# Two-word exponential on VectorE, Q and K through HBM: an attention and long-convolution kernel on one core

## The chip, the cores and the metric

The kernel runs on one core of one Trainium2 chip. The metric is the device time of one execution in microseconds: 822.26 us is the median of three runs (822.12 to 822.35). The engines of the core are named as in the profile: PE (TensorE), DVE (VectorE), ACT (ScalarE), POOL (GpSimd) and SP (SyncE, which here only issues transfers).

## The reference

Two independent halves are computed and laid side by side. S = 2048, D = 640, all tensors bf16.

```python
# half A: short causal filter of k over 4 taps, times v, then a causal long filter per channel
for t in range(4):
    k_shift = k_shift + k_pad[:, t:t + S, :] * shift_k[:, 3 - t]
kv = k_shift * v
y = irfft(rfft(kv, 2S) * rfft(ssm_k, 2S))[:S] + kv * ssm_D
a = q * y
# half B: attention, 32 heads of 20
qkv = x @ wqkv
p = softmax(einsum("bhqd,bhkd->bhqk", q, k) * 20 ** -0.5)
b = einsum("bhqk,bhkd->bhqd", p, v) @ wo
out = concatenate([a, b], axis=-1)
```

## The kernel before

**Attention.** The 32 heads lie in 8 groups of 4. A tile is one group and 512 queries; there are 32 tiles, and a tile has 16 key blocks of 128. One score block is one head, 128 keys and 512 queries: 2,048 of them, numbered in order (four heads, then the next key block). A score block is one matmul with K as weights (L630, 20 x 128) and Q streaming; three neighbouring heads run side by side in three row strips of the array and write three PSUM banks. Banks 0 to 2 and 3 to 5 take turns. ACT turns two or three banks into bf16 exponentials with one instruction (L672), written to a pool of 44 slots of 512 columns (`P_sb`).

Some third banks go to DVE (298 blocks): L692 turns the score into a 16-bit integer that is a rough bf16 power of two (`XV`), and for two such blocks together a chain corrects the mantissa: L727 masks its 7 bits, L728, L729, L730 and L732 form a polynomial, and L722 (both blocks in one instruction) or L724 (one each) adds it to the integer. The result is one bf16 slot.

PV multiplies the exponentials of a key block by V with a column of ones (L750, four heads side by side in four column strips) and sums over the 16 key blocks in bank 6. The tile is copied out (L761), transposed, divided by its sums (L782, L784), and once all groups of a query range are there, multiplied by wo (L831, L847).

**Projections.** x comes transposed by DMA into `xT`. Q and K of one group and 512 positions are one task: five steps of four matmuls side by side (L485) and a copy to `QT` or `KT` (L474); 62 such tasks, and the first two in halves. V of one key block and 8 heads is five matmuls (L531) and a copy (L536): 64 tasks.

**Half A.** The short filter runs on PE with diagonal weights (L560), DVE multiplies by v (L581), and the product kv goes to HBM (`kvr_scratch`), eight transfers of 80 columns for each of 16 row blocks. The long filter is 40 tasks of 128 small matmuls on PE (L1025), 32 to 60 columns each, with windows of the filter loaded from HBM (`hk_load`, 640 transfers) and kv read back (`kvr_load`) and rearranged by POOL (L997). DVE sums (L1041, L1042, L1044), POOL multiplies by q (L1064).

**The order of the work** is written by the builder: `Prog` records each engine's instructions with the semaphores they wait for, and a loop walks along PE's stream. At each point it decides, from costs and ready times that it keeps for all engines, whether the next score group fits, which side task (projection, short filter, output) with a due time to slip in, a convolution piece, PV, or filler matmuls on zeros (`fill`, L391), which are given where PE has streamed too little in the last 3.4 us. `want_vec` decides whether a group's third block goes to DVE. On the chip each engine only follows its list in order.

Of the kernel before, what the change touches and what calls it, by code (L numbers as in the profile page):

```python
# [11 lines left out]
S = 2048  # L12
# [12 lines left out]
NHK = 4  # L25
NAQ = 3
NPU, NPX = 44, 0
# [6 lines left out]
NXB = 3  # L34
KBV, KBW, LONE = 12, 12, 24
CQ, CQD, ZDU = 0.0258, 0.0304, 2.1
KV0, KVS, VQ, CONVE, ZTH, AGE, WAIT3 = 20, 1.7, 5.5, 230, 2.2, 40, 0.2
ZST = 7, 4
DOV, DDEP, SWITCH = 0.085, 0.03, 0.105


EXP_C = (0.07826797, 0.30457564)
# [240 lines left out]
def build_kernel(nc, A_q, A_k, A_v, A_shift_k, A_ssm_k, A_ssm_D, B_x, B_wqkv, B_wo, out):  # L283
# [3 lines left out]
    with ExitStack() as es:  # L287
# [18 lines left out]
        XV_sb = sb("XV", [128, NXB, 1024], U16)  # L306
        XF_sb = sb("XF", [128, 2, 2, 1024])
# [49 lines left out]
        kvr_d = nc.dram_tensor("kvr_scratch", (8, 32, 64, 80), BF16).ap()  # L357

        b_ident, b_ones, b_ZS, b_Dg, b_SK = (Buf() for _ in range(5))
# [5 lines left out]
        b_XF, b_XQ = [Buf(), Buf()], [Buf(), Buf()]  # L365
        b_XV = [[Buf(), Buf()] for _ in range(NXB)]
# [87 lines left out]
        def spare(now):  # L454

            if nu[0] < NPAIR - 6:
                return [MISC] + [OBANK] * (npv[0] == 0 and nu[0] < OBS) + [4, 5]
            side = [2, 5] if nu[0] < NU - 8 and nu[0] >= NPAIR else []
            return side + [MISC] * (not conv_wants(now))
# [7 lines left out]
        npv = [0]  # L467
# [45 lines left out]

        def qs(qc, g):
            return POS[(g, qc)] % NQS
# [7 lines left out]
        VZ = [(0, 8), (8, 8), (16, 8), (24, 8)]  # L523

        def V_task(kb, z, bk):
            h0, nh = VZ[z]
            w = nh * DH
            rd = [b_xT[kb], b_Wa if z == 0 else b_Wb]
            for cc in range(NCC):
                yield (w / 2400 + 0.003, rd if cc == 0 else [])  # L530
                P.op("pe", lambda e, cc=cc: e.matmul(  # L531
                    bank[bk][:, 0:w], xT[:, cc, kb * 128:(kb + 1) * 128],
                    WKV[:, cc, D + h0 * DH:D + h0 * DH + w],
                    start=(cc == 0), stop=(cc == NCC - 1), skip_group_check=True),
                    reads=rd, writes=[bkb[bk]], tok=(cc == NCC - 1), c=w / 2400 + 0.003, st=w / 2400)
            work(1, [(lambda e: e.tensor_copy(V_sb[:, kb, h0 % 16:h0 % 16 + nh, 0:DH],  # L536
                                              bank[bk][:, 0:w].rearrange("p (h d) -> p h d", d=DH)),
                      [bkb[bk], b_ones], [b_V[(kb, z)]], 0.16 + w / 960, False)])
# [11 lines left out]
        def C_task(c, h, bk):  # L550
# [18 lines left out]
            def after():  # L569
                if h < 4:  # L570
                    return
                for t in range(4):
                    bd = Buf()
                    P.dmas("sp", [(ap(kvr_d, [[80, 4], [-5120, 32], [1, 80]], ((32 * n + 31) * 64 + 16 * c + 4 * t) * 80),
                                   kvst[i][:, t, 80 * n:80 * n + 80]) for n in range(8)], d_kvst[4 * i + t], reads=[b_kvst[i]], writes=[bd])
                    b_kvd.append(bd)
                if c < 2:
                    k_load(c + 2)
                    done.add(("L", c + 2))

# [56 lines left out]
        slot, free = {}, set(range(NPX, NPU))  # L637

# [16 lines left out]
        def room(n, vec):  # L655
            a = alloc(n - vec)
            if a is None:
                return None
            if not vec:
                return [a + i for i in range(n)]  # L660
            got = [a + i for i in range(n - vec)]
            free.difference_update(got)
            z = alloc(1)
            free.update(got)
            return None if z is None else got + [z]

        def EXP_task(k, m, vec, b0, got):
            free.difference_update(got)
            for i, z in enumerate(got):
                slot[k + i] = z  # L670
# [4 lines left out]
                reads=[bkb[b0 + i] for i in range(m)], writes=[b_P[z] for z in got[:m]], c=0.066 + 0.4217 * m)  # L675
            if vec:
                chain_start(k + m, b0 + m, got[m])

        chains = []
        xfree = list(range(NXB))  # L680
        nvec = [0, 0]

        opened = []

        def chain_start(n, bk, z):

            nvec[0] += 1
            if not opened:
                opened[:] = [xfree.pop(0), n]
            i, h = opened[0], len(opened) - 2  # L690
            V = XV_sb[:, i, 512 * h:512 * h + 512]
            work(0.2, [(lambda e: e.tensor_scalar(V, bank[bk], scale * 1.4426950408889634 * 128.0, 127.0 * 128.0, op0=ALU.mult,  # L692
                                                  op1=ALU.add), [bkb[bk]], [b_XV[i][h]], 0.684, False)])
            b_P[z].q.append((opened, True))
            opened.append(z)
            if h:
                chain_end()

        def chain_end():

            i, n, zs = opened[0], opened[1], opened[2:]
            opened.clear()
            m = len(zs)
            f = nvec[1] % 2
            nvec[1] += 1
            V, F, Q = XV_sb[:, i, 0:512 * m], XF_sb[:, f, 0, 0:512 * m], XF_sb[:, f, 1, 0:512 * m]
            bv, bf, bq = b_XV[i][0:m], b_XF[f], b_XQ[f]
            a, b = EXP_C
            one, two = 0.154 + 0.1335 * m, 0.154 + 0.267 * m

            def end():
                chains.remove(me)
                xfree.append(i)

# [757 lines left out]
```

## Time and profile before

| what | value |
|---|---|
| median of the runs | 822.26 us |
| profiled execution, its own time | 820.03 us |
| its span | 818.2 us, mean granted clock of PE 0.999 |
| ACT | 800.8 us busy, 750 exponentials (500 of two blocks, 250 of three) |
| DVE | 785.8 us busy, 298 blocks of exponential |
| PE | 796.5 us busy, 11,743 matmuls |
| POOL | 96.4 us busy |
| DMA | 163,226 packets, 121.94 MB, 149 GB/s on average |

A row of the groups reads: line, engine, operation, output and input tile, partitions x elements and type, count, busy us in all, mean ns of one, then the idle time just before these and what ended it. "PEld" is the loading of weights. Successive instructions overlap on an engine, so a mean duration is longer than what one more instruction costs.

### The profile page before, as it was taken

How to read it: one execution, taken by the hardware profiler on the slowest of the kernel's cores; microseconds unless marked ns; L12 is line 12 of the kernel's file. 1: busy time of each engine (PE TensorE's matmuls, PEld its weight loads, DVE VectorE, ACT ScalarE, POOL GpSimd, SP SyncE). 2: the span in 40 equal slices, each digit the busy share in tenths (PEclk: the TensorE clock that was granted, in tenths of full speed). 3: DMA queues.
4: the chain of work that ended last, by engine and by line, in shares of the span. 5: the costliest groups of instructions: out<-in, count | busy, mean ns of one | idle time of the engine just before them, and what ended most of it. 6: DMA issues, size and time to landing. Idle time of an engine off the chain costs nothing.

```text
span 818.2 us, 27604 instructions
## 1 busy us (share of the span) xinstructions
PE 796.5 (97%) x11743; PEld 367.6 (45%) x11743; DVE 785.8 (96%) x1646; ACT 800.8 (98%) x758; POOL 96.4 (12%) x167
## 2 busy tenths in 40 slices
PE   8999999999999999999999999999999999999997
PEld 3444442254545454444454454454444454444332
DVE  2999999999999999999999999999999999999996
ACT  5999999999999999999999999999999999999996
POOL 3000000211010012210001121000111301000110
PEclk9999999999999999999999999999999999999999
DMA  8935423769897889574887778755995968951221
GB/s 181 307 79 94 80 49 52 160 135 195 171 207 159 195 189 204 136 182 111 192 184 165 166 175 190 160 141 118 191 189 135 207 151 180 193 134 46 67 54 37
DMA packets 163226, 121.94 MB, mean 149 GB/s; under 512 B 72832, under 2 KB 161408, under 8 KB 162848
## 3 DMA queue, kind: packets, MB, share of 16 engines
q1 hardware_dynamic: 160912, 117.06, 65.9%
q0 software_dynamic: 736, 2.75, 0.9%
q8 instruction: 93, 1.52, 0.9%
q10 hardware_dynamic: 1456, 0.37, 0.2%
q14 instruction: 29, 0.24, 0.1%
HBM read 106.83 MB, written 10.61 MB: 144 GB/s over the span
## 4 chain that ended last, share of the span: by engine, by line
ACT 43%; DVE 36%; PE 19%; issue 1%; DMA 1%; DVEq 0%
ACT R L672 42%; DVE XV L692 9%; PE PS L630 6%; PE PS L1025 4%; DVE XF L732 4%; DVE XF L729 4%; PE PS L485 3%; DVE R L722 2%; PE PS L750 2%; DVE XF L730 2%; DVE XF L728 2%; DVE XF L727 2%; DVE R L724 2%; DVE R L1044 1%; DVE ZS L1042 1%; DVE ZS L1041 1%
## 5 line engine op out<-in xcount | busy, mean ns | idle before, releaser
L672 ACT ACTIVATE R<-PS 128x1024 bf16<-128x1024 f32 (+1 forms) x750 | 796.6, 1282 | 2.5 <-PE PS L630 1.9
L630 PE MATMUL PS<-QT,KT 20*128 20x512 bf16 x2048 | 291.9, 384 | 10.3 <-ACT R L672 5.5
L692 DVE TENSOR_SCALAR XV<-PS 128x512 uint16<-128x512 f32 x298 | 201.7, 683 | 3.3 <-PE PS L630 1.8
L1025 PEld LDWEIGHTS PS<-R 128*128 128x128 bf16 x5120 | 162.6, 97 | 78.6 <-issue 77.9
L1025 PE MATMUL PS<-R 128*128 128x32 bf16 (+5 forms) x5120 | 196.6, 184 | 0.0
L750 PE MATMUL PS<-R,V_sb 128*21 128x512 bf16 x2048 | 157.5, 383 | 2.6 <-DVE R L722 1.0
L630 PEld LDWEIGHTS PS<-QT,KT 20*128 20x128 bf16 x2048 | 73.0, 91 | 187.9 <-ACT R L672 150.3
L732 DVE TENSOR_TENSOR XF<-XF 128x1024 bf16<-128x1024 bf16 (+1 forms) x155 | 102.5, 661 | 0.3
L729 DVE TENSOR_TENSOR XF<-XF 128x1024 bf16<-128x1024 bf16 (+1 forms) x155 | 102.3, 661 | 0.2
L997 POOL COPY R<-R 128x256 uint32<-128x256 uint32 x80 | 51.1, 639 | 398.5 <-DVE XV L692 144.5
L730 DVE TENSOR_SCALAR XF<-XF 128x1024 bf16<-128x1024 uint16 (+1 forms) x155 | 63.4, 410 | 0.2
L750 PEld LDWEIGHTS PS<-R,V_sb 128*21 128x21 bf16 x2048 | 35.0, 89 | 63.2 <-issue 32.2
L728 DVE TENSOR_SCALAR XF<-XF 128x1024 bf16<-128x1024 uint16 (+1 forms) x155 | 62.4, 407 | 0.2
L727 DVE TENSOR_SCALAR XF<-XV 128x1024 uint16<-128x1024 uint16 (+1 forms) x155 | 62.0, 408 | 0.1
L722 DVE TENSOR_TENSOR R<-XF,XV 128x1024 uint16<-128x1024 bf16 x90 | 61.4, 682 | 0.2
L391 PE MATMUL PS<-Zt 128*128 128x512 bf16 x199 | 58.1, 392 | 1.5 <-DVE Zt L385 1.0
L485 PE MATMUL PS<-xT,WQ 128*20 128x512 bf16 (+1 forms) x660 | 49.6, 375 | 1.7 <-DVE XV L692 0.7
L1064 POOL TENSOR_TENSOR R<-R 128x160 bf16<-128x160 bf16 x64 | 31.2, 487 | 165.1 <-DVE XV L692 48.8
L485 PE MATMUL PS<-xT,WKV 128*20 128x512 bf16 (+1 forms) x660 | 47.9, 375 | 0.1
L724 DVE TENSOR_TENSOR R<-XF,XV 128x512 uint16<-128x512 bf16 x118 | 45.6, 416 | 0.1
L531 PE MATMUL PS<-WKV,xT 128*128 128x160 bf16 x320 | 37.1, 235 | 1.2 <-DVE XV L692 0.8
L531 PEld LDWEIGHTS PS<-WKV,xT 128*128 128x128 bf16 x320 | 21.2, 97 | 22.4 <-issue 11.3
(58 smaller groups left out, 354.7 us busy)
## 6 DMA issues: line engine op xcount, KB each, us to landing
R<-kext_scratch SPq DMA_DIRECT2D x640, 136.0 KB, 3.7
R<-in_A_v_dram SPq DMA_DIRECT2D x4, 640.0 KB, 4.7
kext_scratch<-in_A_ssm_k_dram POOLq DMA_DIRECT2D x1, 2560.0 KB, 13.3
kvr_scratch<-R SPq DMA_DIRECT2D x128, 20.0 KB
R<-kvr_scratch SPq DMA_DIRECT2D x8, 320.0 KB, 5.6
R<-in_A_q_dram SPq DMA_DIRECT2D x32, 80.0 KB, 3.6
out_dram<-R SPq DMA_DIRECT2D x32, 80.0 KB, 3.0
R<-kvr_scratch SPq DMA_DIRECT2D x8, 240.0 KB, 4.9
```

The source lines that it names most:

```text
L485: ins = e.matmul(bank[bk][32 * i:32 * i + DH, 0:n], Wt[:, cc, off + i * DH:off + (i + 1) * DH], xT[:, cc, x0:x0 + n], start=(cc == 0), sto ...
L630: ins = e.matmul(bank[b0 + i], KT[32 * u:32 * u + DH, g % 2, kb * 128:(kb + 1) * 128], QT[32 * u:32 * u + DH, qs(qc, g), :], start=True, s ...
L672: P.op("act", lambda e: e.activation(P_sb[:, s0:s0 + m, :], PS[:, b0 * 512:(b0 + m) * 512].rearrange("p (u q) -> p u q", u=m), ACT.Exp, sc ...
L692: work(0.2, [(lambda e: e.tensor_scalar(V, bank[bk], scale * 1.4426950408889634 * 128.0, 127.0 * 128.0, op0=ALU.mult, op1=ALU.add), [bkb[b ...
L722: last = [(lambda e: e.tensor_tensor(o, Q2, V2, ALU.add), bv + [bq], [b_P[z] for z in zs], two, True)]
L727: (lambda e: e.tensor_scalar(F.bitcast(U16), V, 127, None, op0=ALU.bitwise_and), bv, [bf], one, True),
L728: (lambda e: e.tensor_scalar(Q, F.bitcast(U16), -128.0, None, op0=ALU.add), [bf], [bq], one, True),
L729: (lambda e: e.tensor_tensor(Q, Q, F.bitcast(U16), ALU.mult), [bf, bq], [bq], two, True),
L730: (lambda e: e.tensor_scalar(F, F.bitcast(U16), a / 16384.0, b / 128.0, op0=ALU.mult, op1=ALU.add), [bf], [bf], one, True),
L732: (lambda e: e.tensor_tensor(Q, Q, F, ALU.mult), [bf, bq], [bq], two, True)] + last, end)
L750: ins = e.matmul(bank[OBANK][32 * u:32 * u + DH + 1, :], V_sb[:, kb, (4 * g + u) % 16, :], P_sb[:, slot[4 * b + u], :], start=first, stop= ...
L1025: P.op("pe", lambda e, o=o, lhsT=lhsT, rhs=rhs, st=st, k=k: e.matmul(o, lhsT, rhs, start=st, stop=k == 7, skip_group_check=True), reads=rd ...
```

## The change

- **Exponential on DVE.** The first step writes the 16-bit integer (with another constant) straight into a slot of `P_sb`. For two such blocks together three steps follow: the mantissa with the exponent of 0.5 into `XM`; the exponent with a fixed small mantissa into a second slot; and the first slot times `XM` in place. The sum of the two slots is the exponential; it is never formed, since PV multiplies both by V. `P_sb` has 46 slots, and the block that goes to DVE can be any of the three.
- **PV** is kept as a list per head (`pvq`) and a group takes one item of each head, so that heads with more words than others can be joined freely.
- **Q and K of groups 1 to 6** are computed in chunks of 120 columns (`X_task`: five full matmuls, one copy to `St`), stored to HBM (`qk_scratch`) and loaded back into the four row strips (`KQ_load`). Groups 0 and 7 keep the old tasks.
- **V** of groups 2 to 7 is done for three key blocks in a task and one copy; of groups 0 and 1 for one or two.
- **kv** is stored by whole rows of 640 columns, one transfer for each of 16 row blocks, and loaded in pieces of 80 columns. The loads of the next k and v are issued ahead of the stores.
- Six convolution windows are buffered for four; the constants of the order are others, and the convolution is spread to 160 blocks before the end (230 before). A late side task or convolution piece may be put ahead of a score group.

```diff
-NHK = 4
+NHK = 6
 NAQ = 3
-NPU, NPX = 44, 0
+NPU, NPX = 46, 0
 NQS = 6
 NU = NB * 4
 NPAIR = 8
 VEND = 16
 MM = 0.5
 OBS = 28
-NXB = 3
-KBV, KBW, LONE = 12, 12, 24
+NXB = 2
+KBV, KBW, LONE = 13, 13, 12
 CQ, CQD, ZDU = 0.0258, 0.0304, 2.1
-KV0, KVS, VQ, CONVE, ZTH, AGE, WAIT3 = 20, 1.7, 5.5, 230, 2.2, 40, 0.2
+KV0, KVS, VQ, CONVE, ZTH, AGE, WAIT3 = 20, 1.7, 4, 160, 2.2, 40, 0.6
 ZST = 7, 4
+XG, NXC, NST = 6, 4, 2
+XDL = ((14, 7), (30, 12)), ((70, 8), (90, 12)), ((176, 12), (226, 12)), ((250, 10), (294, 10))
+VBAL = 0
+BEH, BX = 0.5, 0.3
+WAITA, VGAP, SDUE = 0.2, 0, 1.0
 DOV, DDEP, SWITCH = 0.085, 0.03, 0.105
...
-EXP_C = (0.07826797, 0.30457564)
+EXP_C = 127.0 * 128.0 - 76.4457
...
+        def X_task(w, c, t, bk):
+            o = 80 + 120 * c
+            Wt = (WKV, WQ)[w]
+            rd = b_xT[4 * t:4 * t + 4] + [b_Wb] + [b_Wa] * (c == 0)
+            for cc in range(NCC):
+                yield (0.216, rd if cc == 0 else [])
+                P.op("pe", lambda e, cc=cc: e.matmul(bank[bk][0:120, :], Wt[:, cc, o:o + 120], xT[:, cc, 512 * t:512 * t + 512],
+                                                     start=(cc == 0), stop=(cc == NCC - 1), skip_group_check=True),
+                     reads=rd, writes=[bkb[bk]], tok=(cc == NCC - 1), c=0.216, st=0.213)
+            i = nst[0] % NST
+            nst[0] += 1
+
+            def store():
+                P.dma("sp", qk_d[w, 120 * c:120 * c + 120, 512 * t:512 * t + 512], St[0:120, i, :], d_st[i],
+                      reads=[b_St[i]], writes=[b_qk[(w, c, t)]])
+                done.add(("S", w, c, t))
+            work(1, [(lambda e: e.tensor_copy(St[0:120, i, :], bank[bk][0:120, :]), [bkb[bk]], [b_St[i]], 0.69, False)], store)
...
+        def KQ_load(w, g, c):
+            cs = sorted(set((80 * (g - 1) + x) // 120 for x in (0, 79)))
+            ts = range(4) if w == 0 else [c]
+            rd = [b_qk[(w, x, t)] for x in cs for t in ts]
+            pairs = []
+            for u in range(4):
+                r = 80 * (g - 1) + 20 * u
+                dst = KT[32 * u:32 * u + DH, g % 2, :] if w == 0 else QT[32 * u:32 * u + DH, qs(c, g), :]
+                pairs.append((dst, qk_d[w, r:r + 20, :] if w == 0 else qk_d[w, r:r + 20, 512 * c:512 * c + 512]))
+            bw = [b_KT[(g, t)] for t in ts] if w == 0 else [b_QT[qs(c, g)]]
+            P.dmas("sp", pairs, d_kl[g % 2] if w == 0 else d_ql[qs(c, g)], reads=rd, writes=bw)
...
-                for t in range(4):
-                    bd = Buf()
-                    P.dmas("sp", [(ap(kvr_d, [[80, 4], [-5120, 32], [1, 80]], ((32 * n + 31) * 64 + 16 * c + 4 * t) * 80),
-                                   kvst[i][:, t, 80 * n:80 * n + 80]) for n in range(8)], d_kvst[4 * i + t], reads=[b_kvst[i]], writes=[bd])
-                    b_kvd.append(bd)
                 if c < 2:
                     k_load(c + 2)
                     done.add(("L", c + 2))
+                for t in range(4):
+                    bd = Buf()
+                    P.dma("sp", ap(kvr_d, [[D, 4], [-64 * D, 32], [1, D]], (31 * 64 + 16 * c + 4 * t) * D), kvst[i][:, t, :],
+                          d_kvst[4 * i + t], reads=[b_kvst[i]], writes=[bd])
+                    b_kvd.append(bd)
...
+            z, y = zz
+            work(0.2, [(lambda e: e.tensor_scalar(P_sb[:, z, :].bitcast(U16), bank[bk], scale * 1.4426950408889634 * 128.0, EXP_C,
+                                                  op0=ALU.mult, op1=ALU.add), [bkb[bk]], [b_P[z]], 0.684, False)])
...
-                (lambda e: e.tensor_scalar(F.bitcast(U16), V, 127, None, op0=ALU.bitwise_and), bv, [bf], one, True),
-                (lambda e: e.tensor_scalar(Q, F.bitcast(U16), -128.0, None, op0=ALU.add), [bf], [bq], one, True),
-                (lambda e: e.tensor_tensor(Q, Q, F.bitcast(U16), ALU.mult), [bf, bq], [bq], two, True),
-                (lambda e: e.tensor_scalar(F, F.bitcast(U16), a / 16384.0, b / 128.0, op0=ALU.mult, op1=ALU.add), [bf], [bf],
-                 one, True),
-                (lambda e: e.tensor_tensor(Q, Q, F, ALU.mult), [bf, bq], [bq], two, True)] + last, end)
-            me.n = n
-            chains.append(me)
+            work(2, [
+                (lambda e: e.tensor_scalar(M.bitcast(U16), V, 127, 0x3F00, op0=ALU.bitwise_and, op1=ALU.bitwise_or), bv, [bm], one, True),
+                (lambda e: e.tensor_scalar(W, V, 0xFF80, 2, op0=ALU.bitwise_and, op1=ALU.bitwise_or), bv, bw, one, True),
+                (lambda e: e.tensor_tensor(V.bitcast(BF16), V.bitcast(BF16), M, ALU.mult), bv + [bm], bv, two, True)]).n = n
...
+            for it in items:
+                u = next(x for x in us if it in pvq[j][x])
+                pvq[j][u].remove(it)
+                put.append((u, it[0] % NKB, it[1], issued(j, u) and not pvq[j][u]))
 
             def pe(e):
-                for u in range(4):
-                    ins = e.matmul(bank[OBANK][32 * u:32 * u + DH + 1, :], V_sb[:, kb, (4 * g + u) % 16, :],
-                                   P_sb[:, slot[4 * b + u], :],
-                                   start=first, stop=last, tile_position=(0, 32 * u), skip_group_check=True)
+                for u, kb, z, stop in put:
+                    ins = e.matmul(bank[OBANK][32 * u:32 * u + DH + 1, :], V_sb[:, kb, (4 * g + u) % 16, :], P_sb[:, z, :],
+                                   start=first, stop=stop, tile_position=(0, 32 * u), skip_group_check=True)
                 return ins
-            P.op("pe", pe, reads=[b_P[slot[4 * b + u]] for u in range(4)] + [b_V[(kb, zof(g))]],
+            P.op("pe", pe, reads=[b_P[z] for _, z in items] + [b_V[(kb, zof(g))] for kb in sorted(set(x[1] for x in put))],
...
-                P.dma("sp", KVr[b % 2][32 * a:32 * a + 32, 16 * a:64, :].rearrange("p j c -> p (j c)"),
-                      ap(kvr_d, [[5120, 32], [1, (64 - 16 * a) * 80]], 163840 * b), d_kvr[a], reads=b_kvd, writes=[cv["KVr"][b % 2][a]])
+                P.dma("sp", KVr[b % 2][32 * a:32 * a + 32, 16 * a:64, :],
+                      ap(kvr_d, [[64 * D, 32], [D, 64 - 16 * a], [1, 80]], 80 * b), d_kvr[a], reads=b_kvd, writes=[cv["KVr"][b % 2][a]])
 
...
```

## The prediction

> **What bounds the kernel now.** I read the busy shares first, then the groups by shape, the waits, the chain, and single stretches of the timeline. From the page of the profile:
>
> ```profile
> span 818.2 us, 27604 instructions
> ...
> PE 796.5 (97%) x11743; PEld 367.6 (45%) x11743; DVE 785.8 (96%) x1646; ACT 800.8 (98%) x758; POOL 96.4 (12%) x167
> ...
> PEclk9999999999999999999999999999999999999999
> ...
> ACT 43%; DVE 36%; PE 19%; issue 1%; DMA 1%; DVEq 0%
> ```
>
> Three engines are near 97%, and the chain of work that ended last passes between all three. ScalarE (ACT) is the only one whose share is real throughout: it runs from 10.0 to 807 us with 2.5 us of idle time before its exponentials. TensorE's (PE) busy time overstates, since matmul ends are modelled. The groups by shape give the prices (columns: line, engine, operation, shapes, count; busy us, mean ns; idle us before it and what ended it):
>
> ```profile
> L672 ACT ACTIVATE R<-PS 128x1024 bf16<-128x1024 f32 x500 | 491.3, 1134 | 2.4 <-PE PS L630 1.9
> L672 ACT ACTIVATE R<-PS 128x1536 bf16<-128x1536 f32 x250 | 363.9, 1577 | 0.1
> ...
> L692 DVE TENSOR_SCALAR XV<-PS 128x512 uint16<-128x512 f32 x298 | 201.7, 683 | 3.3 <-PE PS L630 1.8
> ...
> L732 DVE TENSOR_TENSOR XF<-XF 128x1024 bf16<-128x1024 bf16 x143 | 97.4, 681 | 0.2
> ...
> L722 DVE TENSOR_TENSOR R<-XF,XV 128x1024 uint16<-128x1024 bf16 x90 | 61.4, 682 | 0.2
> L730 DVE TENSOR_SCALAR XF<-XF 128x1024 bf16<-128x1024 uint16 x143 | 60.0, 421 | 0.1
> ...
> L727 DVE TENSOR_SCALAR XF<-XV 128x1024 uint16<-128x1024 uint16 x143 | 58.6, 419 | 0.1
> L391 PE MATMUL PS<-Zt 128*128 128x512 bf16 x199 | 58.1, 392 | 1.5 <-DVE Zt L385 1.0 <-DVE R L1044 0.4
> ```
>
> Durations overlap: the next instruction starts before the last has ended. What an instruction costs is the time from its start to the next start. Taken so from the trace's start times, where the engine did not idle: ACT 0.923 us for 2 blocks, 1.331 for 3; VectorE (DVE) 0.604 for any 512-wide operation from PSUM, 0.605 for a 1024-wide tensor_tensor, 0.343 for a 1024-wide tensor_scalar. Behind an instruction that needs its predecessor's result it is 0.11 more.
>
> For PE the timeline shows the price of a change of operand shape:
>
> ```profile
> 405.23 0.39 PE L630 MATMUL PS<-QT,KT 20*128 20x512 bf16 x3
> ...
> 405.56 1.04 PE L391 MATMUL PS<-Zt 128*128 128x512 bf16 x4
> ...
> 406.57 0.10 PEld L630 LDWEIGHTS PS<-QT,KT 20*128 20x128 bf16 x3 [0.47 <-ACT R L672]
> ```
>
> Three score matmuls run side by side; the fillers start 0.33 us later. Fillers follow each other at 0.216, so 512 columns are 0.213 and the change of form costs about 0.108. It is paid 1,672 times (counted in the built instruction order).
>
> With these prices I cut the instruction order of the program into 16 parts of 128 score blocks and summed each engine. Totals: ACT 794, DVE 789, PE 733 (552 streaming, 181 changes of form; fillers of 42.5 left out). Taking the largest in each part and adding gives 800.7; the span is 818.2, so 17.5 us are head and tail (10.0 before the first exponential, the rest at the end). Part by part it holds: 50.7 summed against 50.4 in the trace for the second, 49.9 against 49.8 for the third. The fifteenth part has ACT at 50.0, DVE 49.4 and PE 49.2, and took 49.6: a near tie of three engines cost nothing there.
>
> **The change, part by part.**
>
> *Exponential.* ACT gets 1,608 blocks for 1,750, as 615 calls of 2 and 126 of 3: 615 x 0.923 + 126 x 1.331 = 735.3, which is 59 less. DVE takes 440 blocks for 298. Before: 298 x 0.604, 143 chains of 2.233 (L727 to L732), 12 half chains of 1.34, and 90 x 0.607 + 118 x 0.339 for the last step: 610. After: 440 x 0.604, 213 chains of 0.343 + 0.343 + 0.605 = 1.291, 14 half ones of 0.77: 552. Three steps take the place of six, which pays for 142 more blocks and leaves 58 us.
>
> *Two of the three new steps have no exact row.* They mask and OR in one instruction on uint16, and in 73 of 213 chains the two halves of the input stand in descending order of address, in 106 those of the input or of the output of the second mask. L727 is the same mask with one operation, L730 has two operations at the same 0.343. [...] Dropping to half rate costs 0.26 (0.605 for 0.343): on the descending ones 73 + 106 = 179 x 0.26 = 47 us, on all 426 of them 111. I take 0.343, the nearest rows, and keep 47 for the range.
>
> *PV sums two words.* 440 more matmuls of 512 columns. Four run side by side; the order has 635 groups for 512: +123 x 0.213 = +26.2 on PE. The second word's block needs no other work.
>
> *Q and K.* 62 tasks of five 0.213 steps and a 0.602 copy become 14 of the old and 32 of the new kind at the same price: PE -17.0, DVE -9.6. SP issues 152 new transfers (32 stores, 96 + 24 loads). The waits that these add are for a store and a load, queued on SP. K's load of group 1 stands at block 193 and is needed at 256; Q's first at 167 for 256; all later ones have 100 blocks or more. 63 blocks are some 24 us; the loads that this trace shows land in 3 to 7 us. Behind a waiting load on SP stand the convolution's window loads, and behind those PE; a task of four windows comes about every 39 blocks (15 us), and six buffers hold 22 us of them. I cost the latency at nothing; without that cover it would be a store and a load, some 10 us, once per group.
>
> *V.* 64 copies of 0.244 become 30 (11, 4 and 15 of one, two and three blocks: 0.244, 0.408, 0.571 on the line through 160 and 512 columns): 15.6 to 12.9. The matmuls stay.
>
> *kv by rows.* The 128 stores, seen between 54.9 and 139.0 us at 0.5 us of issue each, become 16; nothing on the path waited for them but the convolution's start. In return each load reads 160-byte pieces: 40,960 packets where 1,024 were. [...] By the row, the 160-byte packets of the stores took 18.7 ns in the packet records: 40,960 x 18.7 / 16 = 48 us of each DMA engine's time, against 29 for the long ones, so +19 and, with the stores' 160-byte packets gone, near +5 us on engines that are 66% busy. The load that can hurt is the first: 5,120 packets, 6.0 us instead of about 3.6, and up to 13 if reads at this size take twice the writes. It is set up at block 284 and the first convolution matmul stands at 337, 20 us later, with two POOL copies between; in the present kernel 75 blocks lie there. If it is late, PE stands, and the next scores with it. Between 0 and 8 us, once; I take 2, as most of the 20 us remains.
>
> *Fillers.* 61 for 199: -29.4 on PE. [...] The row: the clock is at full speed throughout, with PE streaming 595 of 818 us, 73%. After, it is 573 of some 770, 74%. So the sum takes no slowing; at half clock PE's 732 would rise above 1,100.
>
> *The sum.* After: ACT 735, DVE 716, PE 732 (560 streaming + 1,599 x 0.108). The largest of each of the 16 parts adds to 750.2. ACT decides nine parts, PE three (first 51.6, ninth 47.6, fifteenth 49.5), DVE four (second 51.6). With the same 17.5: span 767.7. Cut into 32 parts the old order gives 807.5 and the new 754.7, so 52.8 less: 765.4. I take 767, add 2 for the first load and 3 for meetings of three engines that no longer have a slack of 60 us on PE: span 772. The profiled execution was 820.03 for a span of 818.2, and the median of the runs is 822.26, so 4.0 lie around the span: 776.
>
> **The rivals.** *PE becomes the bound* (0.14): what I count as streaming has no room any more, 732 against 735, and nine parts of 16 have PE within 1 us of ACT or above it; each PE stall then makes ACT idle. Before, PE had 85 us to spare and 42.5 of fillers to shift. If each of the 741 score groups waited another 20 to 30 ns: +15 to 22, 791 to 798. Against: the fifteenth part of before.
>
> *New DVE steps at half rate in descending order* (0.10): +47 makes DVE 763, first in nearly every part: about 763 + 17.5 + 10 of meetings + 4 = 794, and up to 800. Without a row for such steps I can't exclude it.
>
> *Out of the packed modes altogether, slower than before* (0.05). [...]
>
> *The change doesn't do what it says* (0.01): the order shows the 440 blocks on DVE; only data could undo that.
>
> **How the numbers follow.** The likeliest case has 0.70: 776, alone 767 to 788. The next two reach to 800, so 766 to 800 leaves out the slow case and the small tails, less than 0.2. About 0.2% is what a measurement of this kernel can tell from no change. All but the slow case and a small part of the PE rival lie below it: faster 0.93, same 0.01, slower 0.06.
>
> **What would show it.** In the profile after: 615 and 126 exponentials with idle time before them below 10 us; 440 conversions; mask-and-OR steps of 0.42 us duration (0.68 would be the half rate, 1.2 the slow case); score matmuls waiting for ACT well below the present value:
>
> ```profile
> PEld PS L630 <- ACT R L672: 150.3, 356, 1.4
> ```
>
> since PE will have less slack; PEclk at 9 throughout; no wait of PE for a load of Q or K, and a wait for POOL or DMA before the first convolution of at most a few us. The prediction is wrong if ACT idles more than 15 us between its first and last exponential, or if a part of the order takes much more than its largest sum.

## The result, and the profile after

The changed kernel takes 788.99 us, the median of 4 runs (782.83 to 808.25); the kernel before took 822.19 beside it. The ratio is 0.957 [0.950, 0.965]. A second set of runs of the same kernel (told last among the experiments) gave 787.54 and 0.957 [0.955, 0.960]. The forecast was 776, with 766 to 800 as its range: the direction and the savings on ACT and DVE held, the engine that sets the time did not, and 11 to 13 us are to be found.

The profiled execution took 792.34 us, with a span of 790.5. The page of the profile after:

```profile
span 790.5 us, 26597 instructions
...
PE 774.0 (98%) x11237; PEld 367.4 (46%) x11245; DVE 719.5 (91%) x1436; ACT 747.1 (95%) x749; POOL 97.2 (12%) x167
...
PEclk9999999999979999999999999999969999999999
DMA  9971438999998887698879878998994978511120
...
q1 hardware_dynamic: 193984, 124.93, 74.2%
...
PE 64%; DVE 19%; ACT 14%; issue 1%; DMA 1%; another core or an unknown queue 0%; SPq 0%; DVEq 0%
```

Before, all three engines stood near 97% and the chain passed between them, 43% of it on ACT and 19% on PE. Now DVE and ACT have dropped by 66 and 54 us of busy time, PE by only 23, and 64% of the chain lies on PE. The clock row, which had 9 in every slice, has a 7 and a 6.

The groups by shape (busy us, mean ns, then the idle time before and what ended it):

```profile
L730 ACT ACTIVATE R<-PS 128x1024 bf16<-128x1024 f32 x615 | 585.1, 1077 | 21.7 <-PE PS L681 20.1
L746 DVE TENSOR_SCALAR R<-PS 128x512 uint16<-128x512 f32 x440 | 296.3, 684 | 27.2 <-PE PS L681 25.8
...
L730 ACT ACTIVATE R<-PS 128x1536 bf16<-128x1536 f32 x126 | 182.7, 1522 | 6.4 <-PE PS L681 6.0
...
L781 DVE TENSOR_TENSOR R<-R,XM 128x1024 bf16<-128x1024 bf16 x213 | 145.7, 684 | 0.8
...
L780 DVE TENSOR_SCALAR R<-R 128x1024 uint16<-128x1024 uint16 x213 | 89.9, 422 | 0.0
L779 DVE TENSOR_SCALAR XM<-R 128x1024 uint16<-128x1024 uint16 x213 | 89.6, 421 | 0.9
```

L779 and L780 are the two mask-and-OR steps: 421 and 422 ns, the duration of the old one-operation mask (419). ACT and DVE now idle 28.1 and 27.2 us, nearly all of it for scores (L681), where before it was 2.5 and 3.3. The waits (engine and line, what it waited for; us in all, times, longest):

```profile
PEld PS L681 <- ACT R L730: 109.8, 267, 1.4
...
ACT R L730 <- PE PS L681: 26.1, 52, 2.3
DVE R L746 <- PE PS L681: 25.8, 37, 4.1
...
POOL R L1055 <- DMA R<-kvr_scratch: 6.8, 1, 6.8
```

Scores wait less for ACT (150.3 before), and ACT waits for scores. Only POOL waited for the first kv load, and no engine waited for a load of Q or K.

Stretches of 3.4 us around the two dips of the clock (columns: stretch, its length, busy us of PE, PEld, DVE, ACT, POOL with counts, granted clock, DMA share, GB/s; the DMA share is the time of all packets over that of 16 engines, 0.72 to 1.23 in these rows; above 1, packets' times overlap):

```profile
221.00:224.40 3.40, 3.08 (x65) 2.01 (x62) 3.37 (x8) 3.40 (x5) 0.00 (x0) 0.99 1.13 223
224.40:227.80 3.40, 3.40 (x51) 1.61 (x47) 2.95 (x7) 2.83 (x3) 0.00 (x0) 0.50 1.23 193
227.80:231.20 3.40, 3.40 (x47) 1.69 (x47) 3.04 (x8) 2.65 (x4) 0.00 (x0) 0.50 1.16 210
231.20:234.60 3.40, 3.40 (x39) 1.14 (x31) 1.41 (x4) 2.73 (x3) 0.64 (x1) 0.50 1.16 222
234.60:238.00 3.40, 3.40 (x70) 1.69 (x62) 2.74 (x6) 2.60 (x4) 0.65 (x1) 1.00 0.72 170
```

```profile
575.90:579.30 3.40, 2.08 (x47) 1.37 (x43) 3.40 (x6) 3.35 (x4) 2.01 (x3) 1.00 1.15 213
579.30:582.70 3.40, 3.37 (x45) 1.65 (x45) 1.96 (x5) 1.77 (x2) 1.12 (x2) 0.51 1.14 221
...
589.50:592.90 3.40, 3.40 (x34) 0.45 (x22) 2.14 (x5) 2.01 (x3) 0.00 (x0) 0.50 1.02 247
592.90:596.30 3.40, 3.40 (x44) 0.98 (x36) 3.13 (x8) 3.22 (x4) 1.60 (x3) 0.99 1.15 224
```

The clock is at half for 10.2 us from 224.4 and for 13.7 us from 579.3; in these two stretches ACT waits 1.9 and 5.3 us for scores, DVE 0.8 and 4.5. In the stretch ahead of each, PE streamed little: counted from the columns of the trace's matmuls, at 0.213 us for 512 (the step from one PV group to the next in this trace) and side-by-side ones once, it is 0.44 and 0.31 of the time, where 0.65 is the median. The timeline of PE (start, length; in brackets the idle time before and what ended it) shows why:

```profile
221.82 0.69 PE L1083 MATMUL PS<-R 128*128 128x32 bf16 x21
222.46 0.39 PE L681 MATMUL PS<-QT,KT 20*128 20x512 bf16 x3
222.79 0.62 PE L1083 MATMUL PS<-R 128*128 128x26 bf16 x16
223.59 0.39 PE L681 MATMUL PS<-QT,KT 20*128 20x512 bf16 x3 [0.18 <-DVE O_norm L841]
223.91 0.65 PE L1083 MATMUL PS<-R 128*128 128x26 bf16 x16
224.49 0.61 PE L681 MATMUL PS<-QT,KT 20*128 20x512 bf16 x3
```

```profile
577.37 0.61 PE L1083 MATMUL PS<-R 128*128 128x32 bf16 x16
579.33 0.77 PE L1083 MATMUL PS<-R 128*128 128x32 bf16 x15 [1.35 <-DMA R<-kext_scratch]
580.03 0.61 PE L681 MATMUL PS<-QT,KT 20*128 20x512 bf16 x3
```

A merged row shows the columns of one of its matmuls; the convolution's have 26 to 60 here, and in the kernel before too. At the first place convolution pieces alternate with scores, and no filler stands between them: PE is busy but streams few columns (54 convolution matmuls and three score groups in the stretch). At the second, PE waited 1.35 us for a filter window from HBM, while the DMA share was 1.15. SP, which issues the loads, was busy all the time there: the four loads of that window went out from 572.6 to 574.5 us, right behind two loads of half A's q that took 2.8 us to issue where two loads of windows take 0.9, and the last landed at 579.3. Right behind, the same score group lasts 0.61 for 0.39.

All nine runs of the changed kernel lie within 1.5 us of one line, span = 779 + 640 x (1 - mean granted clock): 781.2 at 0.998, 785.6 at 0.989, 790.5 at 0.983, 806.5 at 0.957. A hundredth of mean clock costs 6.4 us, and at full clock the span would be 779. Kernels are compared below by this number too ("at full clock": the span less 640 x (1 - clock)). The comparisons leave out executions that stand over 1.5% above the fastest of the same kernel.

### The profile page after: what moved, and what is told of

Same layout as the page of the kernel before. It is cut to its first block, busy times and chain, and to the rows that moved or that the text cites. A ratio compares the mean times of both kernels' runs of the same rounds, so it can differ in the third digit from the quotient of the medians.

```text
span 790.5 us, 26597 instructions
## 1 busy us (share of the span) xinstructions
PE 774.0 (98%) x11237; PEld 367.4 (46%) x11245; DVE 719.5 (91%) x1436; ACT 747.1 (95%) x749; POOL 97.2 (12%) x167
## 3 DMA queue, kind: packets, MB, share of 16 engines
q1 hardware_dynamic: 193984, 124.93, 74.2%
## 4 chain that ended last, share of the span: by engine, by line
PE 64%; DVE 19%; ACT 14%; issue 1%; DMA 1%; another core or an unknown queue 0%; SPq 0%; DVEq 0%
PE PS L681 21%; PE PS L1083 16%; ACT R L730 14%; PE PS L807 12%; DVE R L746 8%; PE PS L529 6%; DVE R L781 3%; PE PS L491 2%; PE PS L581 2%; DVE XM L779 2%; DVE R L780 2%; PE PS L611 2%; DVE R L1102 1%; DVE ZS L1100 1%; PE PS L398 1%; DVE ZS L1099 1%
## 5 line engine op out<-in xcount | busy, mean ns | idle before, releaser
L730 ACT ACTIVATE R<-PS 128x1024 bf16<-128x1024 f32 (+1 forms) x741 | 742.9, 1153 | 28.1 <-PE PS L681 26.1
L746 DVE TENSOR_SCALAR R<-PS 128x512 uint16<-128x512 f32 x440 | 296.3, 684 | 27.2 <-PE PS L681 25.8
L681 PE MATMUL PS<-QT,KT 20*128 20x512 bf16 x2048 | 288.5, 389 | 8.3 <-ACT R L730 2.3
L807 PE MATMUL PS<-R,V_sb 128*21 128x512 bf16 x2488 | 193.4, 389 | 0.5 <-DVE OT_sb L818 0.2
L781 DVE TENSOR_TENSOR R<-R,XM 128x1024 bf16<-128x1024 bf16 (+1 forms) x227 | 151.7, 668 | 1.0
L681 PEld LDWEIGHTS PS<-QT,KT 20*128 20x128 bf16 x2048 | 72.5, 91 | 166.8 <-ACT R L730 109.8
L779 DVE TENSOR_SCALAR XM<-R 128x1024 uint16<-128x1024 uint16 (+1 forms) x227 | 93.6, 412 | 0.9
L780 DVE TENSOR_SCALAR R<-R 128x1024 uint16<-128x1024 uint16 (+1 forms) x227 | 93.9, 414 | 0.0
L529 PE MATMUL PS<-xT,WQ 128*120 128x512 bf16 x80 | 26.4, 404 | 0.0
L529 PE MATMUL PS<-xT,WKV 128*120 128x512 bf16 x80 | 25.6, 402 | 0.2
L539 DVE CAST St<-PS 120x512 bf16<-120x512 f32 x32 | 22.0, 686 | 1.2 <-PE PS L529 0.8
L611 PE MATMUL PS<-R 128*128 128x128 bf16 x320 | 21.7, 220 | 0.0
L904 PE MATMUL PS<-Wo_sb,WKV 128*128 128x128 bf16 (+1 forms) x114 | 20.9, 297 | 0.5 <-issue 0.2
```

What stands on the lines that cost most here:

```text
L529: P.op("pe", lambda e, cc=cc: e.matmul(bank[bk][0:120, :], Wt[:, cc, o:o + 120], xT[:, cc, 512 * t:512 * t + 512], start=(cc == 0), stop=( ...
L611: ins = e.matmul(bank[bk][:, n * 128:(n + 1) * 128], kT[i][:, cc, 16 + 128 * t - j:144 + 128 * t - j], Dg[:, j, cc, :], start=(n + j == 0) ...
L681: ins = e.matmul(bank[b0 + i], KT[32 * u:32 * u + DH, g % 2, kb * 128:(kb + 1) * 128], QT[32 * u:32 * u + DH, qs(qc, g), :], start=True, s ...
L730: P.op("act", lambda e: e.activation(P_sb[:, s0:s0 + m, :], PS[:, b0 * 512:(b0 + m) * 512].rearrange("p (u q) -> p u q", u=m), ACT.Exp, sc ...
L746: work(0.2, [(lambda e: e.tensor_scalar(P_sb[:, z, :].bitcast(U16), bank[bk], scale * 1.4426950408889634 * 128.0, EXP_C, op0=ALU.mult, op1 ...
L779: (lambda e: e.tensor_scalar(M.bitcast(U16), V, 127, 0x3F00, op0=ALU.bitwise_and, op1=ALU.bitwise_or), bv, [bm], one, True),
```

## The experiments

**Theories.** The clock theory: 61 fillers for 199 leave stretches of low streaming, after which PE falls to half clock. The PE theory: PE is full, so what it lacks is room for streaming, fillers and changes of form. The ACT theory is that of the prediction: ACT sets nine parts of 16. The constants `ZLO` and `ZTH` are the streamed us in the last 3.4 us below which the builder gives fillers ahead of a convolution piece, or in idle places; `share(now)` is that sum. Changing them makes the builder write another order, so fillers are not the only thing that moves.

**Fillers: 17, 128 and 217 for 61.**

```diff
-KV0, KVS, VQ, CONVE, ZTH, AGE, WAIT3 = 20, 1.7, 4, 160, 2.2, 40, 0.6
+KV0, KVS, VQ, CONVE, ZTH, AGE, WAIT3 = 20, 1.7, 4, 160, 0.0, 40, 0.6
...
-ZSL, ZLO = 0.3, 1.4
+ZSL, ZLO = 0.3, 0.0
```

> The changed kernel with fillers only at the start: 17 for 61. Clock theory: half-clock stretches come from 3.4 us windows in which PE streams less than about 0.45; with no filler to lift such windows there are more of them, mean granted clock below 0.98 in most runs, median 795 to 815. Rival, PE is simply full and each filler takes its 0.22 us: 44 fewer give back up to 10 us, median 775 to 785, clock as before or no matter.

```diff
-ZSL, ZLO = 0.3, 1.4
+ZSL, ZLO = 0.3, 1.8      (128 fillers)
+ZSL, ZLO = 0.3, 1.9      (217 fillers)
...
                 if behind() and ahead > -BX and can(conv, 9.0, now):
+                    if share(now) < ZLO and over[0] in begun:
+                        fill(now, 1)
                     conv = step(conv)
```

> The changed kernel with a filler ahead of a convolution piece, the late ones too, whenever PE has streamed under 1.8 us in the last 3.4 (1.4 before): 128 fillers for 61. Clock theory: no half-clock stretch past the first 20 us, clock 0.995 or more in every run, runs within 0.3% of each other, median 780 to 786 (the span at full clock of 779 plus a few us for fillers). Rival, PE is full: 67 x 0.22 = 15 us more, median above 795.

> As the one with 128, threshold 1.9 us: 217 fillers. Sum of the largest parts with fillers 778, and head and tail as in the kernel before, so a span near 791 by the sum. Clock theory: clock 0.998, runs alike, median 788 to 794, so no better than the changed kernel but steady. Rival: 156 x 0.22 = 34 us more than the changed kernel, above 815.

| fillers | median us | ratio | clocks of the runs | at full clock |
|---|---|---|---|---|
| 17 | 801.3 | 0.977 [0.975, 0.978] | 0.957 to 0.961 | 771 to 774, extrapolated |
| 61 (the change) | 787.5 | 0.957 [0.955, 0.960] | 0.957 to 0.998 | 779 |
| 128 | 801.7 | 0.979 [0.973, 0.985] | 0.970 to 0.986 | 789 |
| 217 | 814.5 | 0.990 [0.987, 0.994] | 0.987 to 0.998 | 806 |

The clock row of the profiled run with 17 fillers, and below it that with 217:

```profile
PEclk9999998569999999999999999999999999999976
```

```profile
PEclk9999999999999999999999999999999999999999
```

With 17 fillers the clock stays at half for 37.5 us from 134 and for 23.9 us from 765; with 217 it stays full in the profiled run, and the kernel is 27 us slower than with 61. The PE theory holds: a filler costs PE about what it lasts ((806 - 779) / 156 = 0.17 us, some of it other moves of the order), and the medians with 128 and 217 came near what it expected. The clock theory holds one way only. Taking fillers away lowered the clock in all four runs (0.957 to 0.961, where the median of the change is 0.989). Adding them did not secure it: with 128, two stretches of half clock remained (27.3 and 20.5 us) and no run was above 0.986, and with 217 three of four runs had 0.987 to 0.989, where it had expected 0.995 and 0.998. In the profiled run of 217, a further reordering cost its share: twenty matmuls of an output task (L904) and 54 convolution matmuls run in a row from 699.6 to 705.3 us, and ACT waits 6.35 us for the next score.

**The kernel before, with 17 fillers for 199.** Same constants as with 17 above, in the kernel before.

> The kernel before with fillers only at the start: 17 for 199. Clock theory: the fillers are what kept the clock there; without them windows fall under 0.45, clock 0.95 to 0.99, and as PE has some 75 us to spare, only part of it shows: median 825 to 840. Rival: fillers were idle time of PE and do nothing; median 820 to 822, clock 0.999.

It takes 948.63 us (924.32 to 956.36), 127 us more than the kernel before at its side (821.33), with clocks of 0.77 to 0.81, far more than the 825 to 840 of the clock theory:

```profile
PEclk9999995587975769998599555999697655555766
```

The stretches at half clock are 3.4 to 133 us long. So the kernel before needed fillers for its clock. That they cost it nothing is argued, not measured: by the sums of the parts PE had 85 us to spare.

**Convolution matmuls in the wide form.** Half of the 5,120 convolution matmuls can be issued with twice the columns (60 for 30, 56 for 28), with the same result; the builder does so where PE has streamed little (`ZDU`), for 1,758 of 2,560. Here all 2,560 are, and the order is kept, so that PE streams more in the same places.

```diff
+                        if d in (1, 2):
+                            rhs = sub(KVX[i], [[(2 - i) * KVX_E - p, 2], [64, 2], [2, n]], p)
+                            o = sub(bank[MISC], [[-16 if u + x else 16, 2], [256, 2], [1, n]], (4 * u + x) * 16 + d)
```

> The changed kernel, same order on every engine; all 2,560 convolution matmuls for which the order's rule allows it are issued in the form that also adds a row of zeros to the neighbouring output (1,758 were), so 802 matmuls stream twice the columns for some 4.6 ns more each (194 ns against 178 in the groups, overlapping). Clock theory: PE streams some 10 us more in all, windows at 0.45 come above 0.5, so the clock is 0.995 or more in most runs and the median 778 to 785, faster than the changed kernel for more work. Rival, PE is full: 802 x 4.6 ns = 3.7 us slower than the changed kernel, 790 to 796, clock no matter.

789.21 us (783.56 to 817.59), ratio 0.958 [0.955, 0.960]. One run had a clock of 1.000 and a span of 781.8, 2.8 above the changed kernel's line for that clock; the wider matmuls cost 3.7 us by the sums. The profiled run had half clock for 27.3 us from 240.6 and for 54.6 from 588.8, not far from the two places of the change. The clock theory's expectation missed: widening what can be widened does not keep the clock. It could do little at the two places: of the 54 convolution matmuls of the first, 12 were left to widen, of the 37 of the second none (those of 26 and 32 columns have no wide form), and a wait of 1.7 us for a filter window was there in this run too.

**Parts undone.** Q and K back on the old tasks; kv back in pieces (its loads of the next k and v stay ahead of the stores); and both of these and V back, which leaves the exponential, the PV lists, the six windows and the constants of the order. V was not undone alone.

```diff
-XG, NXC, NST = 6, 4, 2
+XG, NXC, NST = 0, 0, 2
...
-                add((4 * kc - 4) if g < 1 else 388 + 2.5 * kc, 1.1, ("K", g, kc),
+                add((4 * kc - 4, 24 + 8 * kc)[g] if g < 2 else 64 * g - 50 + 10 * kc if g < NG - 1 else 388 + 2.5 * kc, 1.1, ("K", g, kc),
```

> The changed kernel with Q and K of all groups by the old tasks (no chunks, no way through HBM). By the sums of the largest part 762.7 for 750.5, so 12 us more at equal clock: 795 to 803; PE has 17 us more and less room for fillers. If the way through HBM costs waits that the sums leave out, it is faster than the changed kernel instead.

```diff
-        kvr_d = nc.dram_tensor("kvr_scratch", (32, 64, D), BF16).ap()
+        kvr_d = nc.dram_tensor("kvr_scratch", (8, 32, 64, 80), BF16).ap()
...
-                    P.dma("sp", ap(kvr_d, [[D, 4], [-64 * D, 32], [1, D]], (31 * 64 + 16 * c + 4 * t) * D), kvst[i][:, t, :],
-                          d_kvst[4 * i + t], reads=[b_kvst[i]], writes=[bd])
+                    P.dmas("sp", [(ap(kvr_d, [[80, 4], [-5120, 32], [1, 80]], ((32 * n + 31) * 64 + 16 * c + 4 * t) * 80),
+                                   kvst[i][:, t, 80 * n:80 * n + 80]) for n in range(8)], d_kvst[4 * i + t], reads=[b_kvst[i]], writes=[bd])
...
-                P.dma("sp", KVr[b % 2][32 * a:32 * a + 32, 16 * a:64, :],
-                      ap(kvr_d, [[64 * D, 32], [D, 64 - 16 * a], [1, 80]], 80 * b), d_kvr[a], reads=b_kvd, writes=[cv["KVr"][b % 2][a]])
+                P.dma("sp", KVr[b % 2][32 * a:32 * a + 32, 16 * a:64, :].rearrange("p j c -> p (j c)"),
+                      ap(kvr_d, [[5120, 32], [1, (64 - 16 * a) * 80]], 163840 * b), d_kvr[a], reads=b_kvd, writes=[cv["KVr"][b % 2][a]])
```

> The changed kernel with the kv store in pieces and loads of long rows as before; the rest of the change kept. Sum of the largest parts 752.3 and 128 fillers, with them 765.8 for 757.6. If the 160-byte loads are what makes convolution windows late (DMA share above 1.0 in the stretches around the wait at 579 us), no PE wait for a window is left, and the DMA share falls; the time by the sums is 784 to 796, slower by the fillers and 112 more issues on SP. Rival, windows are late because of SP's issue alone: the waits stay.

```diff
 (both of the above, and)
-        VKB = ([[kb] for kb in range(8)] + [[8, 9], [10, 11], [12, 13], [14, 15]], [[0], [1, 2, 3], [4, 5, 6], [7, 8, 9], [10, 11, 12], [13, 14, 15]])
+        VKB = ([[kb] for kb in range(16)], [[kb] for kb in range(16)])
```

> The changed kernel with Q and K, V and the kv store as before: what is left of the change is the exponential in two words and the constants of the order. Sum of the largest parts 769.4, 19 more than the changed kernel: 798 to 812 with its losses at the clock. If this is as fast as the changed kernel, the three other parts bring nothing.

| kernel | median us | ratio | fillers' us | parts' sum with fillers + 17.5 | span at full clock |
|---|---|---|---|---|---|
| before | 821.5 | 1 | 42.5 | 822.9 | 818 |
| exponential alone | 819.3 | 0.996 [0.994, 0.998] | 18.7 | 801.5 | 812 |
| without the Q and K part | 801.3 | 0.977 [0.973, 0.981] | 10.0 | 788.2 | 796 |
| without the kv part | 805.9 | 0.980 [0.975, 0.985] | 27.3 | 783.3 | 793 |
| the change | 787.5 | 0.957 [0.955, 0.960] | 13.0 | 775.1 | 779 |

The fifth column is the prediction's method (largest engine of each of 16 parts, plus head and tail), but with the fillers counted on PE; the fillers' us are their number by 0.213. Counted so, all four changed orders end 4 to 11 us above their sum; before, the sum is 5 too high, since there the fillers lay in PE's slack.

The new exponential alone brings 0.4% [0.2, 0.6]: 819.3 us, where 798 to 812 was expected. It takes ACT and DVE down, yet adds PV to PE, which now holds most of the chain. The page of that kernel:

```profile
PE 793.6 (98%) x12031; PEld 367.6 (45%) x12040; DVE 698.5 (86%) x1403; ACT 762.5 (94%) x778; POOL 96.2 (12%) x167
...
PE 65%; ACT 19%; DVE 14%; issue 1%; another core or an unknown queue 0%
```

Q and K in chunks is what makes the room: without it the span at full clock is 17 us longer, the 17.0 that the prediction took off PE for it. Undoing kv costs 14 us at full clock, though it is no work of an engine (805.9 us, where 784 to 796 was expected). Its order has 128 fillers for 61, 14 us more of them, and twenty stand in one row:

```profile
106.66 4.49 PE L398 MATMUL PS<-Zt 128*128 128x512 bf16 x20
111.08 0.39 PE L681 MATMUL PS<-QT,KT 20*128 20x512 bf16 x4
```

ACT waits through them for the next score:

```profile
111.51 4.78 ACT L730 ACTIVATE R<-PS 128x1024 bf16<-128x1024 f32 x5 [4.48 <-PE PS L681]
```

In that stretch (100 to 120 us) ACT is busy 15.1 us, in the changed kernel 18.5. The 128 stores keep SP's queue busy from 57 to 143 us, with the stores and loads of Q and K between them, but no engine waits for a load of Q or K in that trace. So the 14 us are about what the added fillers last. They stand in the written order, whatever has arrived by then; whether the scores behind them could have come earlier is not shown. No wait of PE for a filter window is left, as expected if the 160-byte loads made windows late; but the other rewritten orders have none either, so this doesn't tell the two theories of it apart.

**ACT made faster.** The order is kept; ACT computes 384 of each 512 columns and leaves the rest of the slot as it was, so a part of the exponentials is left out.

```diff
+            wd = 384 if all(z in seen for z in got[:m]) else 512
+            seen.update(got[:m])
-                P_sb[:, s0:s0 + m, :],
-                PS[:, b0 * 512:(b0 + m) * 512].rearrange("p (u q) -> p u q", u=m), ACT.Exp, scale=scale),
+                P_sb[:, s0:s0 + m, 0:wd],
+                PS[:, b0 * 512:(b0 + m) * 512].rearrange("p (u q) -> p u q", u=m)[:, :, 0:wd], ACT.Exp, scale=scale),
```

> The changed kernel with the same order; ACT computes 384 of each 512 columns of its exponentials (the rest of a slot keeps what was in it), so ACT has 571 us for 735. Theory that ACT is still first in most parts and the three engines only meet: what is left is PE with its fillers and DVE, largest parts 750.8 for 757.6, so 7 to 15 us less than the changed kernel at equal clock: spans of 764 to 772 where the clock is above 0.995. Rival, PE alone sets the time and ACT waits for it: less than 4 us of change at equal clock, 775 to 779.

794.67 us (786.53 to 850.49), ratio 0.964 [0.960, 0.967]; at full clock 773 to 775, 4 to 6 below the changed kernel. The groups of this kernel:

```profile
L732 ACT ACTIVATE R<-PS 128x768 bf16<-128x768 f32 x590 | 472.1, 810 | 113.4 <-PE PS L681 97.5
...
L732 ACT ACTIVATE R<-PS 128x1152 bf16<-128x1152 f32 x124 | 137.8, 1130 | 24.1 <-PE PS L681 21.6
```

ACT is busy 112 us less (635.4 for 747.1), and nearly all of it turns into waiting for scores: 141.8 us idle. In the 13 parts that ran at full clock in both traces, the sum fell by some 5 us of 623. That is less than the 7 to 15 of the ACT theory and a little more than the rival's 4. The ACT theory falls: ACT hardly holds the changed kernel back. PE is what the waits point to; DVE was not made faster, so what it holds back beside PE is not told apart.

**Two orders meant to keep the clock.** Other constants of the builder, chosen so that few planned stretches of 3.4 us stream little, with the fillers' line of the 128 and 217 kernels.

```diff
-CQ, CQD, ZDU = 0.0258, 0.0304, 2.1
+CQ, CQD, ZDU = 0.0258, 0.0304, 2.4
-KV0, KVS, VQ, CONVE, ZTH, AGE, WAIT3 = 20, 1.7, 4, 160, 2.2, 40, 0.6
+(A)  20, 1.7, 3.8, 130, 2.0, 40, 0.6
+(B)  20, 1.7, 4.4, 160, 2.2, 40, 0.6
...
-WAITA, VGAP, SDUE = 0.2, 0, 1.0
+(A)  0.35, 0, 1.0
+(B)  0.3, 0, 0.5
...
-DMAX = 2.5
+(A)  3.0
-ZSL, ZLO = 0.3, 1.4
+(A)  0.3, 1.6
+(B)  0.3, 1.65
```

> The changed kernel with the order written under other constants (a filler ahead of a convolution piece, late ones too, where PE has streamed under 1.6 us of 3.4; double-width convolution matmuls below 2.4 us of 2.1; convolution spread to 130 blocks before the end): 50 fillers, and by the order of the matmuls fewer stretches of 3.4 us with under half of it streaming. Sum of the largest parts 750.9, as in the changed kernel. Clock theory: clock 0.995 or more in nearly all runs, median 779 to 785, and runs closer together than the 782.8 to 808.3 of the changed kernel. Rival, the losses are late transfers and a full PE, not low windows: median and spread as in the changed kernel, 785 to 795.

> As keepA with other constants (1.65 us for the filler, 61 fillers, sum of the largest parts 751.3), a second order with few low windows: the same expectations, 779 to 786 by the clock theory, 785 to 795 by the rival.

A: 793.65 us (786.71 to 817.49), ratio 0.962 [0.958, 0.965]; 20.5 us at half clock from 288 in the profiled run, so the clock theory's expectation missed. B: 784.03 us (783.84 to 792.81), ratio 0.958 [0.954, 0.962], as that theory expected. B has 61 fillers like the change, no wait of PE for a filter window, and a clock of 0.997 or more in three of four runs; the change had that in two of nine. At full clock B is at 780 to 781, so its order is no better, and four runs are too few to show that it falls less often. Its median is the lowest of all, but the intervals overlap, and that it beats the change isn't shown.

**The changed kernel again.** No edit.

> The changed kernel once more, unchanged, in five rounds. Clock theory: the spans of the earlier runs lie on a line, 779 us at full clock and 6.4 us more for each per cent of granted clock that is missing (781.0 at 0.997, 806.5 at 0.957); each of the new runs lies within 2 us of it, and the median moves with the clocks that the runs happen to get, between 782 and 800. Rival, the spread has another cause (late transfers, contention) and the clock only goes with it: spans more than 3 us off the line.

787.54 us (783.04 to 788.53), ratio 0.957 [0.955, 0.960]; all five spans are within 1.5 us of the line, as the clock theory expected. The profiled run falls to half clock at the same two places, 10.2 us from 222.2 and 10.2 from 577.2, the second again behind a wait for a filter window (1.0 us). This wait is in the four traces with this order (1.0 to 1.8 us, once, at 577 to 589 us), and in none with another order of the changed kernel.

## Why the prediction was right and wrong

*Right, with its numbers.* ACT made 615 and 126 calls and DVE 440 conversions. The new DVE steps ran at the rows taken for them (419 and 421 ns) in the 213 chains, descending addresses included: 421 and 422 ns in the mean, 414 of the 426 under 450, so both rivals on DVE are out, and the 47 us kept for them with it. The half rate, 0.26 us more, and the 1.2 us that mark the slow case were estimates; no run shows either as the price of these steps, whose means are 421 to 424 ns wherever the profile lists them by shape. Q and K gave PE about what was worked out. Short packets of kv took 20.7 ns each where 18.7 was taken. The first kv load cost PE nothing; 2 was put down.

*DMA time.* Near 5 us more of each DMA engine were put down, for kv. The queue's share rose from 65.9% of 818.2 us to 74.2% of 790.5, which is 47 us more. Without the Q and K part it is 32 us less than that, without the kv part 8: the packets of Q and K were left out, since that part was priced by its waits alone. The trace shows no wait for a load of Q or K; what a fuller queue did to the filter window of 579 us isn't told apart from SP's order of issue.

*"So the sum takes no slowing"* (the fillers). This step failed. It compared averages, 73% and 74% of PE streaming (the count by columns alone gives less, 0.65 in the median stretch), and an average can't tell of a clock that falls for 10.2 and 13.7 us after single poor stretches of 3.4: those before the falls streamed 0.44 and 0.31, with PE busy 3.08 and 2.08 of 3.40 us. In the traces here, what counts is how much is streamed in each single window. The runs' clocks (median 0.989) put 7 us on the median run, and the profiled run paid some 8 us in the two parts that hold the falls, the fifth (some 48.5 us for a sum of 45.3) and the twelfth (some 52 for 47.1).

*"Fillers of 42.5 left out" of PE.* That was right for the kernel before, where counting them makes the sum too high. It was carried over to an order in which PE has no slack: counted, they add 7.1 us to the sum of the largest (757.6 for 750.5; the prediction's own sum was 750.2).

*"ACT decides nine parts", and 3 us for meetings.* With PE at 732 against ACT's 735, "a near tie cost nothing" was argued from one part of before. The fourteen parts at full clock ran 11.8 us over their sums, 0.8 each, a good part of it the fillers. The PE rival described the bound rightly and priced it too high for the full clock (791 to 798 for 779 + 2). By the prediction's own sign, over 15 us of idle ACT, ACT was not the bound: it idles 28.1. So the likeliest case named the wrong engine; with ACT's sum and PE's 3 us apart, that alone cost its time little.

*Queued behind SP.* The prediction named the line from a waiting load to the filter windows to PE and costed it at nothing. SP did stand three times behind a store of Q or K, 9.1 us in all, at 100 to 400 us, and no window was late there. PE waited once, for 1.35 us, behind slow issues of q. Its price was less the wait than the 13.7 us at half clock that followed; that the wait brought the fall fits the 0.31, but was not tested alone.

The sum put right: 757.6 + 17.5 + 4 of meetings = 779 at full clock, + 7 for the clock + about 2 around the span (792.34 for 790.5) = 788. The 4.0 around the span was a median's distance to one profiled execution, and 2 of it were not there. That the result lies in the range is in part luck: the likeliest case alone went to 788, the room up to 800 was made for half-rate DVE steps and a PE bound, and it took in a loss at the clock that the prediction put at nothing.

*Left open.* Why a fall lasts 3.4 us once and 54.6 another time isn't settled: PE is busy throughout, and what it streams tells only in part: of the half-clock stretches of 3.4 us with 0.44 or more, 19 of 72 were followed by full clock, of those below 7 of 137. The undone parts are new orders with other fillers, so their differences are those of an order. More filter windows in flight would test the second place directly; it wasn't tried.

## What to carry to other kernels

When an edit uses up the slack of an engine, everything that this slack paid for (fillers, short waits, changes of form) enters the sum at full price: here 61 fillers added 7.1 us to the sum of the largest, where before the 42.5 us of 199 lay in PE's slack. Judge PE's clock by the poorest 3.4 us of the order (0.44 and 0.31 streamed before the two falls here), not by its mean streaming (74%), and look for stretches of many narrow matmuls or a short wait for a load: a 1.35 us wait was followed by 13.7 us at half clock. Where an engine waits, look first at what the other one runs meanwhile: without the kv part, ACT waited for twenty fillers, not for a load. An instruction-saving edit on two engines is worth what the third has room for: alone it brought 0.4%, with room made on PE it brought 4.3%.

## What the runs showed of the hardware

- In these traces the clock stays at half for multiples of 3.41 us (stretches of 3.41, 10.24, 13.65, 20.48, 27.31, 34.13, 37.55, 54.61 us). Between 25 and 760 us of the fourteen traces, 26 windows at full speed were followed by one at half speed: 25 of them had PE streaming 0.24 to 0.49 of the time, one (in the kernel without the Q and K part) 0.56. Of the 2,801 that were followed by another at full speed, the lowest had 0.41 and only fifteen had less than 0.50. Put together: below 0.40 all 15 fell, from 0.40 to 0.50 ten fell and fifteen did not, above it one of 2,787 fell. So in these traces the fall goes with what is streamed in a window, near 0.40 to 0.50 of it; in the two windows before the falls of the change PE was busy 3.08 and 2.08 of 3.40 us.
- In the half-clock windows of the change PE is busy all the time (3.37 to 3.40 of 3.40 us), but gets through only 0.41 to 0.44 of full-speed columns (0.25 to 0.52 over all traces, in the middle 0.42).
- A tensor_scalar of two bitwise operations on uint16, 128x1024 between SBUF tiles, takes 0.42 us like one with a single operation (421 and 422 ns in the change, 419 before), in descending order of its two halves too.
